# A two-layer attention and Mish-MLP block: norms handed out in eleven steps, heads inverted at other steps, two loads behind the attention

## The chip, the cores and the metric

The kernel runs on one core of a Trainium2 chip. The metric is the device time of one execution in microseconds (us), lower is better. A core has TensorE (PE, matmuls), VectorE (DVE), ScalarE (ACT), GpSimd (POOL) and SyncE (SP, which here only issues DMAs); each engine works through its own instructions in order, and they meet through semaphores.

## The reference

```python
def reference(A_x, A_wqkv, A_wo, B_x, B_w1, B_b1, B_w2):
    def _A_ref(x, wqkv, wo):
        ...
        scores = jnp.einsum("bhqd,bhkd->bhqk", q, k) * (Dh ** -0.5)
        p = _softmax(scores, axis=-1)
        o = jnp.einsum("bhqk,bhkd->bhqd", p, v)
        return (lambda x, *d: x.transpose(*d))(o, 0, 2, 1, 3).reshape(B, S, D) @ wo
    def _B_ref(x, w1, b1, w2):
        h = jnp.einsum("bsd,df->bsf", x, w1) + b1
        sp = jnp.log1p(jnp.exp(-jnp.abs(h))) + jnp.where(h > 0, h, jnp.zeros_like(h))  # stable softplus
        act = h * jnp.tanh(sp)
        return jnp.einsum("bsf,fd->bsd", act, w2)
    x = A_x
    x = x + _A_ref(_layernorm(x, axis=-1), A_wqkv, A_wo)
    x = x + _B_ref(_layernorm(x, axis=-1), B_w1, B_b1, B_w2)
    x = x + _A_ref(_layernorm(x, axis=-1), A_wqkv, A_wo)
    x = x + _B_ref(_layernorm(x, axis=-1), B_w1, B_b1, B_w2)
    return x
```

S = 2048 rows of D = 512, 32 heads of 16, F = 1792 hidden features, all float32. Both layers use the same weights.

## The kernel before, in words

**Tiles.** The 2048 rows are four tiles c = 0 to 3 of 512. Operands of the projections are split into a high and a low part in a reduced format (th and tl for a normed tile, oh and ol for an attention output, ah and al for an activation, two halves of every weight), and three matmuls replace one (`mm3`, L177). Weights are split once, in layer 0, kept in DRAM and loaded again as whole 1 MB tiles (`ready`, L159).

**The shared pool.** `b8` (L95) hands out tiles from one pool of 22 slots: q and k rows, the exponentials p, the heads' num and rec, oh and ol, weights, residuals x2 and normed tiles all take slots of it. A tile that takes a slot waits until the last reader of the tile before it is done, and a load that waits so holds the DMA queue that it stands in. Normalised rows on their way to DRAM and back share three buffers named raw.

**Order.** A scheduler places the instructions by a simulated time line. The kernel chains all matmuls of a stage in the order in which it writes them (`att.pe`) and pins others with `behind` (L118), which keeps pinned instructions of an engine in the program's order; an instruction that isn't pinned may be placed elsewhere.

**The stages of a layer.** Projections to q, k and v (`qkv`); attention over 8 groups of 4 heads and 4 query tiles; the output projection; the MLP. Attention is a loop of STEPS = 512 steps (`run`, L489): each works on 4 heads of 128 keys, in items P and S (scores of two heads or one, and their exponentials, L438 and L448), M (two matmuls for the running row maximum of a later step, and a VectorE reduce, L390) and v (p times v, L463). Maxima run 22 steps ahead, so they end 22 steps before the loop does. In the value projections before the loop a maximum is interleaved by `some_max`, at every third step. `hooks` is a table from step to functions that run behind that step's items; "STEPS-14" is the hook 14 steps before the end.

**The heads' way out** (`HeadsOut`, L630), for each row tile c: `load` brings the sums den and the outputs num back from DRAM (4 + 8 DMAs on SyncE), `invert` takes the reciprocal on VectorE (L647) and stores it through POOL's queue (4 DMAs, rscr, L649), `spread` loads it broadcast (8 DMAs on POOL's queue, rec, L655), `parts` multiplies (L659), casts on POOL (oh, L662) and subtracts (ol, L663), all 128x2048. For c = 0 to 2 these hang on hooks of the loop's last 42 steps. Tile 3 ends with the loop: its last output `ot` is stored by SyncE (L487) and loaded after the loop, inverted in the middle of projection 2, and `pieces` does its product and split in halves (L673, L674, L678) on the MLP's features 2 to 5.

**The output projection** (`wo_parts`, L681) has 16 steps of three matmuls a tile. Tiles 0 and 1 run whole, tile 2 for 10 steps (HEAD), with the first MLP norm (`norm_parts`, by PE transposes) drawn in between; the rest of tile 2 and all of tile 3 run inside the MLP. VectorE adds each half tile to the residual x2 (L701), which `load_res` has loaded.

**The MLP** (`mlp`, L705) goes over 4 tiles x 14 features: `hid` makes a hidden feature tile (12 matmuls) and a chain of ten ScalarE and VectorE operations over it, `outp` the output two features later (12 matmuls). Hooks here are keyed (c, f). The norm of the next row tile is made beside it by `norm_blocks` (L267), drawn by `spread` (L300) in six parts on six features in a row: statistics of all four subtiles; scaling, transposes and 4 DMAs of one half; the same of the other half; the load of the turned tile; two halves of the split (ScalarE L295, VectorE L296). In layer 0's last row tile three norms for the next layer's q and k are drawn as well, from features 1, 5 and 8.

Of the kernel before, what the change touches and what calls it, by code (L numbers as in the profile page):

```python
# [9 lines left out]
F32 = mybir.dt.float32  # L10
F32R = mybir.dt.float32r
BF16 = mybir.dt.bfloat16
AF = mybir.ActivationFunctionType
# [5 lines left out]
P = 128  # L19
# [31 lines left out]
MAX_M = (6, 3, 7)  # L51
T_BUFS = {"he": 1, "hr": 1}
NBLK = 22


def units(done):
# [12 lines left out]
def kernel(ctx: ExitStack, tc: tile.TileContext, x, wqkv, wo, w1, b1, w2, out):  # L69
# [48 lines left out]
    def behind(ins):  # L118
        return tc.keep_in_program_order(ins)
# [61 lines left out]
            pe(nc.tensor.matmul(acc, ah, bl, start=False, stop=False))  # L181
            pe(nc.tensor.matmul(acc, al, bh, start=False, stop=last and i == n - 1))  # L182

    def statistics(src, nm):
        st = tmp.tile([P, NCH, 6], F32, tag="st", name=f"st{nm}")
        mv = tmp.tile([P, NCH, 2], F32, tag="mv", name=f"mv{nm}")
        ve = tmp.tile([P, NCH], F32, tag="ve", name=f"ve{nm}")
        rs = tmp.tile([P, NCH], F32, tag="rs", name=f"rs{nm}")
        for t in range(NCH):
            behind(nc.vector.bn_stats(st[:, t], src[:, t]))  # L190
            behind(nc.vector.bn_aggr(mv[:, t], st[:, t]))
        nc.gpsimd.tensor_scalar(ve, mv[:, :, 1], EPS, None, op0=ALU.add)
        nc.gpsimd.tensor_tensor(rs, ve, mhalf, op=ALU.pow)
        return rs, mv

    def norm_parts(src, nm, got, key, tag, fine=False, pin=lambda ins: ins, pe=lambda ins: ins, halves=False):
        st = tmp.tile([P, NCH, 6], F32, tag="st", name=f"st{nm}")
        mv = tmp.tile([P, NCH, 2], F32, tag="mv", name=f"mv{nm}")
# [65 lines left out]
    def grouped(t):  # L264
        return t.rearrange("p (g j r) -> p g j r", j=2, r=TR)

    def norm_blocks(src, nm, got, key):  # L267
        rs, mv = statistics(src, nm)
        yield
        th = b8([P, KT, CW], F32R, f"th{nm}")  # L270
        tl = b8([P, KT, CW], F32R, f"tl{nm}")
        got[key] = (th, tl)
        raw = tl.bitcast(F32)
        turned = dram.tile([D, CW], F32, name=f"nt{nm}")
        for h in range(2):
            xn = tmp.tile([P, 2, D], F32, tag="raw", name=f"xn{nm}{h}", bufs=3)
            for j in range(2):
                t = h + 2 * j
                nc.vector.tensor_scalar(
                    xn[:, j], src[:, t], mv[:, t, 0:1], rs[:, t : t + 1], op0=ALU.subtract, op1=ALU.mult  # L280
                )
            y = tmp.tile([P, D // TR, 2, TR], F32, tag="raw", name=f"y{nm}{h}", bufs=3)
            for j in range(2):
                nc.vector.transpose(y[:, :, j], xn[:, j].rearrange("p (b r) -> p b r", r=TR))
            for a in range(P // TR):
                n0 = h * CW // 2 + a * 2 * TR
                nc.sync.dma_start(
                    turned[:, n0 : n0 + 2 * TR].rearrange("(b q) n -> q b n", q=TR),
                    y[ts(a, TR)].rearrange("q b j r -> q b (j r)"),
                )  # L290
            yield
        nc.sync.dma_start(raw, turned.rearrange("(k p) n -> p k n", p=P))
        yield
        for k in range(KT):
            nc.scalar.activation(th[:, k], raw[:, k], AF.Copy)  # L295
            nc.vector.tensor_tensor(tl[:, k], raw[:, k], th[:, k].bitcast(F32), op=ALU.subtract)  # L296
            if k % 2:
                yield

    def spread(hooks, c, f0, src, nm, got, key):  # L300
        parts = norm_blocks(src, nm, got, key)
        for i in range(6):
            hooks.setdefault((c, f0 + i), []).append(lambda: next(parts, None))

    class Attention:
        def __init__(self, l, scr):
# [231 lines left out]
    def qkv(l, att, wts, tt, order, within, due):  # L538
        scr = att.scr
        ahead = [0]  # L540

        def some_max():
            if ahead[0] < AHEAD + PRE:
                for n in range(2):
                    att.max_mm(ahead[0], n)
                ahead[0] += 1

        done = 0
        spare = []
        parts = iter(())  # L550
        for n, (m, c) in enumerate(order):
            for fn in within.get((n, 0), []):
                fn()
            w = wts[m // 2]
            if n % 2:
                if not spare:
                    two = b8([P, 2, 2, CW], F32R, f"pt{l}{m}{c}")
                    spare += [two[:, 0], two[:, 1]]
                pt = spare.pop(0)
            else:  # L560
                pt = tmp.tile([P, 2, CW], F32R, tag="raw", name=f"pt{l}{m}{c}", bufs=3)
            th, tl = tt[c]
            acc = pbank("s", f"qk{l}{c}{m}")
            if l == 0 and n < 2:
                for i, (part, t) in enumerate(((0, th), (0, tl), (1, th)) if n else ((0, th), (1, th), (0, tl))):
                    for k in range(KT):
                        start, stop = i == k == 0, i == 2 and k == KT - 1
                        att.pe(nc.tensor.matmul(acc, w[:, part, k, ts(m % 2, P)], t[:, k], start=start, stop=stop))
            for k in range(KT if l or n > 1 else 0):
                for fn in within.get((n, k), []) if k else []:  # L570
                    fn()
                mm3(
                    acc,
                    [(w[:, 0, k, ts(m % 2, P)], w[:, 1, k, ts(m % 2, P)], th[:, k], tl[:, k])],
                    first=k == 0,
                    last=k == KT - 1,
                    pe=att.pe,
                )
            split_psum(pt[:, 0], pt[:, 1], acc)
            nc.scalar.dma_start(  # L580
                scr[m][:, :, ts(c, CW)].bitcast(F32).rearrange("a p n -> p a n"), pt.bitcast(F32)
            )
            for fn in due.get((m, c), []):
                fn()
            for _ in range(2):
                next(parts, None)
            if m in (0, 4):
                done += 1
                if done == 2 * NCH:
                    parts = att.prep_qk(0)  # L590
                    for _ in range(2 * PREP):
                        next(parts)
            elif done == 2 * NCH and m in MAX_M:
                some_max()
        i = 0
        for c in range(NCH - 1):
            for _ in v_parts(l, c, wts, tt, att, False):
                i += 1
                if i % 3 == 2:
                    some_max()  # L600

    def v_parts(l, c, wts, tt, att, paired):
# [214 lines left out]
    for l in range(2):  # L817
# [24 lines left out]
        def load_res(c):  # L842
            x2 = b8([P, NCH, D], F32, f"x2{l}{c}")
            nc.sync.dma_start(x2, xsrc[ts(c, CW), :].rearrange("(t p) d -> p t d", p=P))
            x2s.append(x2)
# [9 lines left out]
        def at(s, fn):  # L855
            hooks.setdefault(s, []).append(fn)
# [6 lines left out]
                split_keep(hooks, 20 + 26 * i, key, *src)  # L863
        for i in range(2):
            at(STEPS - 9 + 2 * i, lambda i=i: wot.append(ready(f"wo{i}", l)))
            at(STEPS - 5 + 2 * i, lambda i=i: load_res(i))
        at(STEPS - 1, lambda: load_w1(0))
        outs = [HeadsOut(l, c, att.oscr) for c in range(NCH)]
        for c, (t0, t1, t2, t3) in enumerate(((-42, -21, -20, -14), (-26, -20, -19, -12), (-10, -6, -5, 0))):
            o = outs[c]  # L870
            at(STEPS + t0, o.load)
            at(STEPS + t1, o.invert)
            at(STEPS + t2, o.spread)
            at(STEPS + t3, lambda o=o: o.parts())
# [3 lines left out]

        att.run(hooks, v_parts(l, NCH - 1, wts, tt, att, True))
        outs[3].load()  # L880
        load_res(2)
        load_res(3)
        load_w1(1)
        load_w2(0)
        for _ in project(0):
            pass
        first = norm_parts(x2s[0], f"m{l}0", tts, 0, "s", pin=behind, pe=att.pe, halves=True)
        for i, _ in enumerate(project(1)):
            for n in range({0: 1, 8: 1, 11: 2, 14: 2}.get(i, 0)):
                next(first)  # L890
        last = project(2)
        for i in range(HEAD):
            next(last)
            for n in range({1: 2, 6: 1}.get(i, 0)):
                next(first)
            if i == 3:
                outs[3].invert()
                outs[3].spread()
        load_w1(2)
        load_w2(1)  # L900
        hooks = {}
# [16 lines left out]
            on(f1, lambda i=i: load_w1(i))  # L918
            on(f2, lambda i=i: load_w2(i - 1))
        on(9, lambda: load_w2(6))  # L920
        for c in range(NCH - 1):
            spread(hooks, c, 5 if c else 7, x2s[c + 1], f"m{l}{c + 1}", tts, c + 1)
        wts, tt = {}, {}
        if l == 0:
            end = NCH - 1
            for f, js in ((2, (0,)), (4, (2,)), (9, (1,)), (11, (3,)), (12, (4,)), (13, (5,))):
                hooks.setdefault((end, f), []).append(lambda js=js: load_qkv(1, wts, js, splits))
            for c in range(end):
                spread(hooks, end, (1, 5, 8)[c], x2s[c], f"q1{c}", tt, c)
        mlp(l, x2s, w1t, w2t, tts, xs if l == 0 else out, hooks, att.pe, last)  # L930
    close_banks()

# [27 lines left out]
```

## Time and profile before

| | us |
|---|---|
| median of 3 runs (lowest to highest) | 3543.35 (3543.12 to 3545.58) |
| the profiled execution | 3551.37 |
| its span in the profile | 3549.6 |

The profile is of one execution. Its times run from the span's start. A row of a group of instructions gives the line, the engine, the operation, what it writes and reads, the count, the busy time with the mean of one in ns, and the idle time of the engine just before them with what ended it. PE's ends are modelled, so overlapping matmuls show as 0.39 us each where one starts every 0.23 us. "Granted clock" is the share of TensorE's full clock.

| stage | layer 0, us from the start | layer 1 |
|---|---|---|
| q, k, v | 0 to 163 | 1790 to 1931 |
| attention | 163 to 1410 | 1931 to 3179 |
| output projections 0 to 2 | 1410 to 1444 | 3179 to 3211 |
| MLP | 1444 to 1790 | 3211 to 3545 |

### The profile page before, as it was taken

What the parts mean: (1) busy time and instruction counts of PE and PEld (TensorE: products, weight loads), DVE (VectorE), ACT (ScalarE), POOL (GpSimd) and SP (SyncE); (2) the same over time, 40 slices, a digit from 0 to 9 for tenths busy, and PEclk for the clock granted to TensorE, in tenths of its full rate; (3) what the DMA queues carried; (4) which work ended last, traced back from release to release, by engine and by line L of the source; (5) the groups of instructions that cost most, each with busy time, mean ns of one, the idle gap of its engine ahead of it and who ended that gap; (6) DMA issues with size and microseconds to landing.
All of it is one profiled execution on the core that took longest, in us unless ns stands there. A gap on an engine that the chain in (4) does not pass through costs nothing. (4 is left out here: it accounts for less than half of the span.)

```text
span 3549.6 us, 68828 instructions
## 1 busy us (share of the span) xinstructions
PE 3503.1 (99%) x28572; PEld 1932.6 (54%) x28572; DVE 3003.6 (85%) x3164; ACT 2578.2 (73%) x3515; POOL 242.9 (7%) x392
## 2 busy tenths in 40 slices
PE   9999999999999999899999999999999999999999
PEld 7644444444444444788776444444444444447887
DVE  6699999999999994577856999999999999945775
ACT  3288888888888887356522888888888888863665
POOL 3100001010000002100010000000000000020000
PEclk9999999999999999999999999999999999999999
DMA  7631322213132115621374211112111111165210
GB/s 247 228 92 47 83 52 69 56 55 71 44 80 50 41 21 119 193 72 47 107 236 153 48 34 43 38 29 44 32 35 37 43 35 29 21 136 180 80 36 24
DMA packets 182196, 273.97 MB, mean 77 GB/s; under 512 B 67508, under 2 KB 111476, under 8 KB 168060
## 3 DMA queue, kind: packets, MB, share of 16 engines
q1 hardware_dynamic: 154964, 192.91, 21.5%
q10 hardware_dynamic: 19176, 43.06, 3.5%
q0 software_dynamic: 7744, 33.60, 3.4%
q8 instruction: 224, 3.67, 0.5%
q14 instruction: 88, 0.72, 0.1%
HBM read 158.87 MB, written 109.58 MB: 76 GB/s over the span
## 5 line engine op out<-in xcount | busy, mean ns | idle before, releaser
L390 DVE TENSOR_REDUCE mxv<-pm 128x2 f32<-128x1024 f32 x2048 | 2383.3, 1219 | 144.6 <-PE pm L386 95.8
L438 ACT ACTIVATE p<-sp 128x1024 f32<-128x1024 f32 x1366 | 1395.7, 1022 | 18.4 <-DVE num L659 10.2
L463 PE MATMUL pv<-p,va 128*32 128x256 f32 (+2 forms) x16032 | 1169.6, 393 | 0.4 <-ACT ot L484 0.2
L386 PE MATMUL pm<-ks,qs 48*128 48x512 f32 x4096 | 1099.4, 447 | 1.6 <-DVE mxv L390 1.6
L448 ACT ACTIVATE p<-ss 128x512 f32<-128x512 f32 x1364 | 815.3, 598 | 344.7 <-PE ss L447 248.4
L437 PE MATMUL sp<-qs,ks 50*128 50x512 f32 x2732 | 741.5, 445 | 0.0
L386 PEld LDWEIGHTS pm<-ks,qs 48*128 48x128 f32 x4096 | 452.1, 184 | 351.3 <-issue 175.4
L463 PEld LDWEIGHTS pv<-p,va 128*32 128x32 f32 x16032 | 369.0, 109 | 502.9 <-issue 424.2
L447 PE MATMUL ss<-qs,ks 50*128 50x512 f32 x1364 | 613.1, 450 | 11.0 <-ACT p L448 11.0
L447 PEld LDWEIGHTS ss<-qs,ks 50*128 50x128 f32 x1364 | 252.5, 185 | 342.4 <-ACT p L448 235.0
L437 PEld LDWEIGHTS sp<-qs,ks 50*128 50x128 f32 x2732 | 270.4, 184 | 184.2 <-ACT p L438 110.2
L405 POOL CAST np<-nt 128x32 fp32r<-128x32 f32 x64 | 13.4, 210 | 2215.1 <-DVE nt L403 2215.1
L719 ACT ACTIVATE hb<-h,b1t 128x512 f32<-128x512 f32 x112 | 77.1, 689 | 94.3 <-PE h L182 91.7
L174 ACT ACTIVATE pt<-qk 128x512 fp32r<-128x512 f32 x64 | 38.3, 598 | 141.8 <-PE qk L182 101.5
L723 ACT ACTIVATE hr<-he 128x512 f32<-128x512 f32 x112 | 70.9, 633 | 89.6 <-DVE he L722 89.6
L726 DVE TENSOR_TENSOR hb<-hb,hr 128x512 f32<-128x512 f32 x112 | 77.2, 689 | 45.8 <-ACT hr L724 43.2
L729 ACT ACTIVATE ah<-hb 128x512 fp32r<-128x512 f32 x112 | 70.4, 629 | 57.5 <-DVE hb L726 44.3
L730 DVE TENSOR_TENSOR al<-hb,ah 128x512 fp32r<-128x512 f32 x112 | 77.2, 689 | 41.2 <-ACT ah L729 30.2
L720 DVE TENSOR_SCALAR he<-hb 128x512 f32<-128x512 f32 x112 | 47.6, 425 | 75.0 <-ACT hb L719 74.4
L722 DVE SCALAR_TENSOR_TENSOR he<-he 128x512 f32<-128x512 f32 x112 | 77.1, 688 | 21.0 <-ACT he L721 20.8
L175 DVE TENSOR_TENSOR pt<-qk,pt 128x512 fp32r<-128x512 f32 x64 | 43.9, 685 | 52.0 <-ACT pt L174 51.9
L721 ACT ACTIVATE he<-he 128x512 f32<-128x512 f32 x112 | 70.5, 629 | 22.7 <-DVE he L720 22.6
(237 smaller groups left out, 3090.8 us busy)
## 6 DMA issues: line engine op xcount, KB each, us to landing
scr<-pt ACTq DMA_DIRECT2D x64, 512.0 KB
qs<-scr SPq DMA_DIRECT2D x174, 128.0 KB
ks<-scr SPq DMA_DIRECT2D x174, 128.0 KB
vscr<-v SPq DMA_DIRECT2D x32, 512.0 KB
va<-vscr SPq DMA_DIRECT2D x64, 256.0 KB
oscr<-ot SPq DMA_DIRECT2D x64, 256.0 KB
ww<-sw POOLq DMA_DIRECT2D x14, 1024.0 KB, 4.6
num<-oscr SPq DMA_DIRECT2D x64, 128.0 KB
```

The costliest lines, as they stand in the source:

```text
L386: nc.tensor.matmul(pm[:, e], qs[u][rows, q0 : q0 + P], ks[u][rows, ts(n, 512)], start=True, stop=True)
L390: nc.vector.tensor_reduce(self.mxs[b][:, 2 * u : 2 * u + 2, qt, n], pm, axis=AX.X, op=ALU.max)
L437: self.pe(nc.tensor.matmul(sp[:, e], k, q, start=True, stop=True))
L438: nc.scalar.activation(self.pts[-1][:, 0:n], sp[:, 0:n], AF.Exp, scale=SCALE)
L447: self.pe(nc.tensor.matmul(sp, k, q, start=True, stop=True))
L448: nc.scalar.activation(self.pts[i // 3][:, 2], sp, AF.Exp, scale=SCALE)
L463: nc.tensor.matmul(self.accs[b][ts(h, VW), cols], self.va[b // NCH][:, kt, h, :], self.pts[j][:, e, cols], start=kt == 0 and q0 == 0, stop ...
L719: nc.scalar.activation(hb, acc, AF.Identity, bias=b1t[:, f : f + 1])
L722: nc.vector.scalar_tensor_tensor(e, e, 2.0, e, op0=ALU.add, op1=ALU.mult)
L723: nc.scalar.activation(r, e, AF.Ln, bias=1.0, scale=0.5)
L726: nc.vector.tensor_tensor(hb, hb, r, op=ALU.mult)
L730: nc.vector.tensor_tensor(low, full, high.bitcast(F32), op=ALU.subtract)
```

## The change

It has five parts. (1) `norm_blocks` becomes `norm_units`: the same operations, now all of VectorE's and ScalarE's pinned, in eleven units: four of statistics, four of scaling and transposing one subtile (the second and the fourth also issue 4 DMAs), the load, two halves of the split. Two tables say on which feature tile, counted 0 to 55 through the four row tiles, each unit runs. The slots for th and tl are taken at the load, no longer at the first scaling. (2) The hooks of load, invert, spread and parts of tiles 0 to 2 move; tile 3 is inverted and spread at step 6 of projection 1, no longer at step 3 of projection 2. (3) Of the loads, only residual 0 stays inside the loop; residual 1 and the first w1 tile go behind the loop and behind tile 3's load, and the order of the others changes. (4) The maxima in the value projections come one step later. (5) `statistics` goes into `norm_units`.

```diff
+M_NORMS = (
+    (3, 4, 5, 6, 6, 7, 8, 9, 10, 11, 11),
+    (14, 14, 15, 17, 18, 19, 20, 21, 22, 24, 25),
+    (31, 31, 32, 32, 32, 33, 34, 35, 36, 38, 39),
+)
+Q_NORMS = (
+    (22, 22, 23, 23, 26, 27, 28, 29, 43, 45, 48),
+    (36, 36, 37, 37, 40, 41, 42, 43, 50, 52, 53),
+    (46, 46, 47, 47, 48, 49, 50, 51, 53, 54, 55),
+)
...
-    def norm_blocks(src, nm, got, key):
-        rs, mv = statistics(src, nm)
-        yield
+    def norm_units(src, nm, got, key):
...
+        for t in range(NCH):
+            behind(nc.vector.bn_stats(st[:, t], src[:, t]))
+            behind(nc.vector.bn_aggr(mv[:, t], st[:, t]))
+            if t == NCH - 1:
+                nc.gpsimd.tensor_scalar(ve, mv[:, :, 1], EPS, None, op0=ALU.add)
+                nc.gpsimd.tensor_tensor(rs, ve, mhalf, op=ALU.pow)
+            yield
+        turned = dram.tile([D, CW], F32, name=f"nt{nm}")
+        for h in range(2):
+            xn = tmp.tile([P, 2, D], F32, tag="raw", name=f"xn{nm}{h}", bufs=3)
+            y = tmp.tile([P, D // TR, 2, TR], F32, tag="raw", name=f"y{nm}{h}", bufs=3)
+            for j in range(2):
+                t = h + 2 * j
+                behind(
+                    nc.vector.tensor_scalar(
+                        xn[:, j], src[:, t], mv[:, t, 0:1], rs[:, t : t + 1], op0=ALU.subtract, op1=ALU.mult
+                    )
+                )
+                behind(nc.vector.transpose(y[:, :, j], xn[:, j].rearrange("p (b r) -> p b r", r=TR)))
+                if j:
+                    for a in range(P // TR):
+                        n0 = h * CW // 2 + a * 2 * TR
+                        nc.sync.dma_start(
+                            turned[:, n0 : n0 + 2 * TR].rearrange("(b q) n -> q b n", q=TR),
+                            y[ts(a, TR)].rearrange("q b j r -> q b (j r)"),
+                        )
+                yield
         th = b8([P, KT, CW], F32R, f"th{nm}")
         tl = b8([P, KT, CW], F32R, f"tl{nm}")
...
         nc.sync.dma_start(raw, turned.rearrange("(k p) n -> p k n", p=P))
         yield
         for k in range(KT):
-            nc.scalar.activation(th[:, k], raw[:, k], AF.Copy)
-            nc.vector.tensor_tensor(tl[:, k], raw[:, k], th[:, k].bitcast(F32), op=ALU.subtract)
+            behind(nc.scalar.activation(th[:, k], raw[:, k], AF.Copy))
+            behind(nc.vector.tensor_tensor(tl[:, k], raw[:, k], th[:, k].bitcast(F32), op=ALU.subtract))
             if k % 2:
                 yield
 
-    def spread(hooks, c, f0, src, nm, got, key):
-        parts = norm_blocks(src, nm, got, key)
-        for i in range(6):
-            hooks.setdefault((c, f0 + i), []).append(lambda: next(parts, None))
+    def spread(hooks, when, src, nm, got, key):
+        parts = norm_units(src, nm, got, key)
+        for at in when:
+            hooks.setdefault(divmod(at, FT), []).append(lambda: next(parts))
...
-                if i % 3 == 2:
+                if i % 3 == 0:
                     some_max()
...
-            at(STEPS - 5 + 2 * i, lambda i=i: load_res(i))
-        at(STEPS - 1, lambda: load_w1(0))
+        at(STEPS - 4, lambda: load_res(0))
         outs = [HeadsOut(l, c, att.oscr) for c in range(NCH)]
-        for c, (t0, t1, t2, t3) in enumerate(((-42, -21, -20, -14), (-26, -20, -19, -12), (-10, -6, -5, 0))):
+        for c, (t0, t1, t2, t3) in enumerate(((-42, -38, -36, -21), (-26, -23, -22, -17), (-13, -9, -8, -1))):
...
         outs[3].load()
+        load_res(1)
+        load_w1(0)
         load_res(2)
+        load_w2(0)
+        load_w1(1)
         load_res(3)
-        load_w1(1)
-        load_w2(0)
...
             for n in range({0: 1, 8: 1, 11: 2, 14: 2}.get(i, 0)):
                 next(first)
+            if i == 6:
+                outs[3].invert()
+                outs[3].spread()
         last = project(2)
         for i in range(HEAD):
             next(last)
             for n in range({1: 2, 6: 1}.get(i, 0)):
                 next(first)
-            if i == 3:
-                outs[3].invert()
-                outs[3].spread()
...
-        for c in range(NCH - 1):
-            spread(hooks, c, 5 if c else 7, x2s[c + 1], f"m{l}{c + 1}", tts, c + 1)
+        for c, when in enumerate(M_NORMS):
+            spread(hooks, when, x2s[c + 1], f"m{l}{c + 1}", tts, c + 1)
...
-            for c in range(end):
-                spread(hooks, end, (1, 5, 8)[c], x2s[c], f"q1{c}", tt, c)
+            for c, when in enumerate(Q_NORMS):
+                spread(hooks, when, x2s[c], f"q1{c}", tt, c)
```

More of the change, by code (lines that the diff above doesn't have):

```diff
@@ L182, in mm3 @@
             pe(nc.tensor.matmul(acc, al, bh, start=False, stop=last and i == n - 1))
[L184 to L194, printed above, removed]
     def norm_parts(src, nm, got, key, tag, fine=False, pin=lambda ins: ins, pe=lambda ins: ins, halves=False):
@@ L265, in grouped @@
         return t.rearrange("p (g j r) -> p g j r", j=2, r=TR)
-    def norm_blocks(src, nm, got, key):
-        rs, mv = statistics(src, nm)
-        yield
+    def norm_units(src, nm, got, key):
+        st = tmp.tile([P, NCH, 6], F32, tag="st", name=f"st{nm}")
+        mv = tmp.tile([P, NCH, 2], F32, tag="mv", name=f"mv{nm}")
+        ve = tmp.tile([P, NCH], F32, tag="ve", name=f"ve{nm}")
+        rs = tmp.tile([P, NCH], F32, tag="rs", name=f"rs{nm}")
+        for t in range(NCH):
[25 more added lines that the diff above has]
+                yield
         th = b8([P, KT, CW], F32R, f"th{nm}")
@@ L273, in norm_blocks @@
         raw = tl.bitcast(F32)
[L274 to L291, printed above, removed]
         nc.sync.dma_start(raw, turned.rearrange("(k p) n -> p k n", p=P))
```

## The prediction

> **What bounds the kernel now.** I read the page's totals first, then the waits of TensorE, then busy time and granted clock stage by stage.
>
> ```profile
> span 3549.6 us, 68828 instructions
> ...
> PE 3503.1 (99%) x28572; PEld 1932.6 (54%) x28572; DVE 3003.6 (85%) x3164; ACT 2578.2 (73%) x3515; POOL 242.9 (7%) x392
> ...
> L390 DVE TENSOR_REDUCE mxv<-pm 128x2 f32<-128x1024 f32 x2048 | 2383.3, 1219 | 144.6 <-PE pm L386 95.8
> ```
>
> TensorE is busy for 3503.1 of 3549.6 us. No matmul is added or removed, so the change can only move the rest: time in which PE waits, and time in which it runs at a lower clock. The reduce row says who leads in the attention: VectorE waits for PE there (95.8 us over 2048 reduces).
>
> The waits of TensorE (total us, times, longest):
>
> ```profile
> PE mo L742 <- ACT ah L729: 13.0, 4, 4.6
> PE ss L447 <- ACT p L448: 11.0, 4, 5.5
> PE wo L182 <- DVE ol L678: 6.9, 2, 3.4
> PE wo L180 <- DVE x L701: 3.6, 2, 2.6
> PE pm L386 <- DVE mxv L390: 1.6, 2, 0.8
> ```
>
> Five causes hold 36.1 us. Where they lie (stretch, then PE, PEld, DVE, ACT, POOL busy, granted clock, DMA share, GB/s):
>
> ```profile
> 1386.80:1410.30 23.50, 17.97 (x179) 6.86 (x171) 5.45 (x3) 14.55 (x20) 7.97 (x13) 0.85 0.90 237
> 1410.30:1444.30 34.00, 31.38 (x147) 25.11 (x143) 18.61 (x24) 2.99 (x5) 5.27 (x7) 1.00 0.73 210
> 1444.30:1531.00 86.70, 78.36 (x329) 63.87 (x330) 50.73 (x84) 39.54 (x62) 5.37 (x10) 0.96 0.56 171
> 1636.00:1712.00 76.00, 76.00 (x337) 62.96 (x336) 55.41 (x97) 46.12 (x73) 2.03 (x2) 1.00 0.15 42
> 1712.00:1790.00 78.00, 72.05 (x304) 58.44 (x303) 62.33 (x117) 43.19 (x71) 5.83 (x6) 0.96 0.55 165
> 3153.00:3177.00 24.00, 19.21 (x158) 7.28 (x162) 5.45 (x3) 15.35 (x22) 7.97 (x13) 0.79 0.95 239
> 3211.40:3300.00 88.60, 81.31 (x333) 66.14 (x334) 51.62 (x86) 40.39 (x63) 5.38 (x10) 0.92 0.53 165
> ```
>
> The first three are layer 0's end of attention, projections and first MLP tile; then its third and fourth MLP tiles; then layer 1's end of attention and first MLP tile. An undisturbed MLP tile keeps PE busy for all its 76.00 us. The others lose idle time, and clock besides: seven stretches run at half clock, each begun by one of the long waits.
>
> ```profile
> 1392.70:1399.40 6.70, 5.07 (x30) 1.79 (x30) 3.16 (x2) 5.42 (x7) 3.02 (x4) 0.50 0.51 173
> ...
> 3256.40:3263.10 6.70, 5.62 (x13) 4.46 (x14) 2.32 (x3) 0.10 (x1) 0.00 (x0) 0.50 0.47 159
> sum 43.50, PE 38.72 PEld 23.90 DVE 24.55 ACT 24.34 POOL 5.44; mean PE 5.53 PEld 3.41 DVE 3.51 ACT 3.48 POOL 0.78
> ```
>
> In them PE works 38.72 us, of which half, 19.4 us, is lost. So about 36 + 19, some 55 us or 1.6%, is all that this change can win.
>
> **The change part by part.** First the heads of tiles 0 to 2, at the end of attention. VectorE in order of time, layer 0:
>
> ```profile
> 1358.24 1.77 DVE L647 RECIPROCAL den<-den 128x128 f32<-128x128 f32 x2
> 1373.68 2.29 DVE L659 TENSOR_TENSOR num<-num,rec 128x2048 f32<-128x2048 f32 x1 [13.68 <-DMA rscr<-den]
> 1381.91 2.29 DVE L663 TENSOR_TENSOR ol<-num,oh 128x2048 fp32r<-128x2048 f32 x1 [5.93 <-POOL oh L662]
> 1390.39 2.29 DVE L659 TENSOR_TENSOR num<-num,rec 128x2048 f32<-128x2048 f32 x1 [6.19 <-DMA num<-oscr]
> 1394.82 2.29 DVE L663 TENSOR_TENSOR ol<-num,oh 128x2048 fp32r<-128x2048 f32 x1 [2.14 <-POOL oh L662]
> 1397.03 0.95 DVE L647 RECIPROCAL den<-den 128x128 f32<-128x128 f32 x1
> 1416.11 2.29 DVE L659 TENSOR_TENSOR num<-num,rec 128x2048 f32<-128x2048 f32 x1 [18.13 <-PE wo L182]
> 1420.55 2.29 DVE L663 TENSOR_TENSOR ol<-num,oh 128x2048 fp32r<-128x2048 f32 x1 [2.14 <-POOL oh L662]
> ```
>
> ```profile
> 1392.77 1.02 ACT L438 ACTIVATE p<-sp 128x1024 f32<-128x1024 f32 x1 [5.57 <-DVE num L659]
> ```
>
> Here p is the exponential's tile, num the product and rec the spread reciprocal. Two reciprocals run back to back, and their chains (four rscr issues, a landing, eight rec issues, a landing, the product) go through POOL one after the other, so tile 1's product starts at 1390.39. An exponential needs a slot of the shared pool and gets it when that product ends, after 5.57 us; PE's longest "ss" wait is this one. With tile 0 inverted at STEPS-38, its 1 reciprocal, 12 POOL issues and later POOL cast are out of the way, and tile 1's chain runs alone. Tile 2's chain shows what it takes alone: 1397.03 to 1416.11, 19.1 us. From 1359.1 (second of the pair) tile 1's product would start at 1378.2 and end at 1380.5, while the exponential asks for the slot at 1392.77 - 5.57 = 1387.2: 6.7 us to spare. What goes is the idle time of the two stretches, 5.53 + 4.79, and half of the matmul time at half clock, 2.5 in layer 0 and, by 24.00 x 0.21, about 5.0 in layer 1: 17.9 us. Bounds 0 and 17.9; I take 16, near the top, as the margin exceeds the wait itself.
>
> Tile 2's reciprocal sits behind tile 1's product in VectorE's order. With that product 12.2 us sooner and the hook three steps sooner, I put it at 1385, its product at 1404 and ol (starting 4.44 later, by the last two rows) done by 1411. Attention would end at 1410.3 - 5.53 - 2.5 = 1402.3. Tile 2's load also moves three steps up, but reads what SyncE stores just ahead of it: nothing.
>
> The residual adds queue behind that ol, and PE waits for them, 3.6 us in both layers. In the projections 42 steps of three matmuls take 31.38 us, 0.75 each, so the second one wants its bank at 1402.3 + 12.0 = 1414.3; the add would end at 1412. Bounds 0 and 3.6; taken 3.
>
> Tile 0's reciprocal, 0.95 us, now lies among the reduces of the last block, where VectorE has 144.6 idle us in 2048 gaps. Bounds 0 and 0.95 a layer; taken 0.45, together 0.9 lost.
>
> Next tile 3's heads, and the loads. SyncE's queue in layer 0, and POOL and VectorE on what follows:
>
> ```profile
> 1418.43 0.34 SPq L164 DMA_DIRECT2D w10l<-ww  x1
> 1418.87 0.38 SPq L644 DMA_DIRECT2D num<-oscr  x1
> 1419.34 0.38 SPq L487 DMA_DIRECT2D oscr<-ot  x1
> ...
> 1426.38 1.94 SPq L641 DMA_DIRECT2D den<-oscr  x2
> ```
>
> ```profile
> 1441.09 2.08 POOL L649 DMA_DIRECT2D rscr<-den  x4 [11.32 <-DVE den L647]
> 1448.69 1.55 POOL L655 DMA_DIRECT2D rec<-rscr  x3 [5.52 <-DMA rscr<-den]
> ```
>
> ```profile
> 1470.97 1.23 DVE L673 TENSOR_TENSOR num<-num,rec 128x1024 f32<-128x1024 f32 x1 [7.89 <-DMA rec<-rscr]
> ```
>
> The first w1 load waits for tile 2's product (ends 1418.40), and behind it stands the store of the last attention output, 9 us after the loop's end at 1410.3. Moved behind tile 3's load, w1 and residual 1 hold nothing up: the store goes at about 1403, den 7 us later as now, at 1410. The reciprocal moves 13 steps up, to 1402.3 + 23 x 0.75 = 1419.5; its rscr issue at 1420.8. From rscr to product took 1441.09 to 1470.97, 29.9 us, which gives 1450.7. The product is wanted at 1470.97 - 7.89 = 1463.08, less the 8.0 and 2.6 gained, 1452.5. So the wait that starved PE twice (mo, then wo) is gone by only 1.8 us. At stake in the two first MLP tiles: idle 8.34 + 7.29, and of the 19.4 us of half clock what is left beside 2.5, 5.0 and 3.1 (78.00 x 0.04, fourth tile), 8.8: 24.4 us. Bounds 0 and 24.4; taken 17, because the margin is thin and the same weights still share the DMA engines.
>
> Residual 1 and w1 are now issued at about 1412 (0.4 us each of SyncE); the residual is first read half way through the second projection, 1402.3 + 24 x 0.75 = 1420.3. I cost them at nothing while that holds; the projections hide them.
>
> Then the norms. Their instructions stay the same in number; they are pinned and handed out one feature tile at a time. In layer 0's fourth tile three norms of the next layer meet: VectorE 62.33 busy us in 78, against 55.41 in 76, and
>
> ```profile
> 1765.81 0.63 ACT L295 ACTIVATE thq<-tlq 128x512 fp32r<-128x512 f32 x1 [4.38 <-DMA tlq<-ntq]
> ```
>
> ScalarE stands for 4.38 us before a split whose load has not landed. The change moves nearly all of two norms' statistics, scaling and transposes into the second and third tiles (the third's VectorE has 20 us free), and puts two feature tiles between load and split for tile 1. Idle 5.95 and clock 3.1 are at stake: bounds 0 and 9.0, taken 7.5. Pinning itself: a split that comes too early blocks ScalarE for later feature tiles. Bounds 0 and what the second rival says; taken 2 lost.
>
> Last, running maxima one step later in the value projections: the reduce before has one more step of three matmuls, some 0.75 us, to finish in, against two waits of 0.8. Bounds 0 and 1.6, taken 1.4.
>
> Sum: 16 + 3 - 0.9 + 17 + 7.5 - 2 + 1.4 = 42.0 us. The profiled execution took 3551.37 us with a span of 3549.6, the median of the runs shown is 3543.35; I take the saving off the median: **3501 us**.
>
> **The rivals.** *Tile 3's product stays late.* Loads that come sooner keep the engines full just then, and 1.8 us is nothing beside this spread:
>
> ```profile
> DMA to landing us min/median/max: 3.5/6.3/18.3
> ```
>
> The 17 stay lost: 25 us gained, 3518. For it the slowest rec landing, 18.3 us; against it the other landings' median, 6.3.
>
> The Trainium skill, page "DMA: Bandwidth & Descriptors", section "Queues, rings and completion order", says each DMA engine takes turns between the queues packet by packet, so POOL's megabyte would not wait behind SyncE's weights. At its 358 GB/s two megabytes take 5.9 us, an estimate from that page; by it this rival's chance would be 0.05 and the time still 3501. The 18.3 us here speak against so short a share.
>
> *Slower: pinned splits block.* One mechanism: a split whose load is late holds ScalarE, and every feature tile behind it. The 4.38 us wait is followed by the stage's longest idle time, at most 5.95, and its half clock, 3.1; I price it at 6.5, some 70% of both. Nine norms pay it if loads land after the splits' places: 58.5 lost, 42 + 2 gained, 3558. It turns the sign from the seventh norm on. For it: half of tile 1's split in the MLP comes a feature tile sooner. Against it: all other splits keep their distance from the load or get a feature tile more.
>
> *The wait moves.* Residual 1 lands after 1420.3; the add, the first norm's scaling and PE's transposes stand behind it. Eight us late with half clock behind it is 12 a layer: 3501 + 24 = 3525. For it: at the attention end's 237 GB/s a megabyte takes 4.4 us, and it is second after tile 3's own, 1421 from 1412.
>
> *The slot is another's.* The exponential may get a slot with a later release; then the 16 stay lost: 3517. Against it: the exponential's row names that product, and it starts 0.1 us after its end.
>
> **How the numbers follow.** Forecast 0.50, with its own range 3490 to 3508 (all 55 gained, and the taken sum less 7); product late 0.18; wait moves 0.13; other slot 0.11; slower 0.08. The range reaches from 3489 to 3527 to take in the three middle cases and leaves out the slower one and pairs of them. A difference under 0.2%, 7 us, can't be told from none: pairs of the middle cases come there, 0.06; so faster 0.86, slower 0.08.
>
> **What would show it.** Right: no "ss" wait on p near either layer's attention end, tile 1's product near 1378; the store of the last output issued within 2 us of the loop's end; product L673 starting without a DMA wait; clock 1.00 in the stretches above; the fourth MLP tile without idle PE. Wrong: L673 still waiting on rec; transposes L257 waiting behind residual 1; "mo" waits beside a pinned split in MLP tiles that had none.

## The result, and the profile after

| | before | after |
|---|---|---|
| median of 6 runs each, taken together (lowest to highest), us | 3544.47 (3540.85 to 3548.10) | 3527.52 (3526.25 to 3534.03) |
| the profiled execution, us | 3551.37 | 3526.25 |
| its span, us | 3549.6 | 3524.4 |

The ratio is 0.9955, with a 95% interval from 0.9943 to 0.9968: faster by 17 us, where 42 were forecast. The 3527.52 us lie just above the range's 3527, and the forecast of 3501 is 26 us off.

From here on the line numbers are those of the changed kernel: the lines of before named here stand 10 further down. TensorE's work and its waits (total us, times, longest) in the profile after; "pv" is p times v, "ss" the scores of one head, "mo" the MLP's output, "wo" the output projection and "pm" the running maxima:

```profile
span 3524.4 us, 68795 instructions
...
PE 3492.5 (99%) x28572; PEld 1925.5 (55%) x28572; DVE 3003.6 (85%) x3164; ACT 2575.0 (73%) x3515; POOL 239.2 (7%) x392
```

```profile
PE pv L473 <- ACT p L448: 10.2, 2, 5.7
PE wo L192 <- DVE ol L688: 8.1, 2, 4.0
PE ss L457 <- ACT p L458: 1.7, 3, 0.8
```

Of the five waits of before, those of "mo" for ah and of "wo" for the residual sums are gone, and that of "pm" for the maxima is down from 1.6 us to 0.4. The wait of "ss" for an exponential is mostly gone by name only: "pv" now waits for one, for 10.2 us, and "ss" still for 1.7, where it was 11.0. "wo" for ol is larger than before. Stage by stage (stretch, then PE, PEld, DVE, ACT, POOL busy, granted clock, DMA share, GB/s; the same five parts of layer 0 as before, then the half-clock stretches):

```profile
1386.10:1409.40 23.30, 18.76 (x186) 7.39 (x182) 4.59 (x2) 15.20 (x21) 5.96 (x9) 0.89 0.59 178
1409.40:1440.90 31.50, 31.50 (x143) 25.80 (x143) 13.89 (x22) 2.99 (x5) 7.88 (x14) 0.97 0.95 314
1440.90:1527.60 86.70, 82.38 (x355) 67.38 (x354) 53.90 (x89) 42.42 (x66) 1.28 (x2) 0.98 0.48 146
1622.90:1698.90 76.00, 75.81 (x335) 62.48 (x334) 60.29 (x110) 45.68 (x74) 3.08 (x4) 1.00 0.25 70
1699.60:1777.60 78.00, 77.82 (x344) 64.09 (x343) 60.02 (x106) 46.22 (x77) 2.23 (x4) 1.00 0.49 159
```

```profile
1404.30:1411.10 6.80, 5.21 (x22) 2.56 (x23) 2.72 (x2) 3.03 (x4) 1.89 (x1) 0.50 0.02 6
...
3233.80:3237.20 3.40, 3.40 (x10) 2.63 (x9) 2.37 (x6) 0.00 (x0) 0.23 (x1) 0.51 0.81 270
sum 20.50, PE 15.56 PEld 9.00 DVE 11.44 ACT 5.68 POOL 5.30; mean PE 3.89 PEld 2.25 DVE 2.86 ACT 1.42 POOL 1.33
```

The fourth MLP tile went from 72.05 busy us in 78 to 77.82, and the first from 78.36 of 86.70 to 82.38. The attention's end is as it was: 18.76 busy of 23.30, against 17.97 of 23.50. What the two long waits left cost, in both layers together, is 10.2 + 8.1 us of waiting and half of the 15.56 at half clock, some 26 us. That this is also the distance to the forecast is in part chance, as the part on the prediction shows. They are these, the exponential of the last pair but one in each layer and the projection of tile 3 (here in layer 0):

```profile
1404.81 1.02 ACT L448 ACTIVATE p<-sp 128x1024 f32<-128x1024 f32 x1 [5.94 <-DVE num L669]
...
3157.57 1.02 ACT L448 ACTIVATE p<-sp 128x1024 f32<-128x1024 f32 x1 [7.08 <-DVE num L669]
```

```profile
1481.52 0.50 PE L192 MATMUL wo<-wo1l,ol 128*128 128x512 f32 x1 [4.04 <-DVE ol L688]
```

And VectorE and POOL on the way to the first:

```profile
1373.57 2.29 DVE L669 TENSOR_TENSOR num<-num,rec 128x2048 f32<-128x2048 f32 x1 [2.05 <-DMA rec<-rscr]
1378.00 2.29 DVE L673 TENSOR_TENSOR ol<-num,oh 128x2048 fp32r<-128x2048 f32 x1 [2.13 <-POOL oh L672]
1380.21 0.94 DVE L657 RECIPROCAL den<-den 128x128 f32<-128x128 f32 x1
1402.43 2.29 DVE L669 TENSOR_TENSOR num<-num,rec 128x2048 f32<-128x2048 f32 x1 [21.28 <-DMA rec<-rscr]
```

```profile
1381.45 1.99 POOL L659 DMA_DIRECT2D rscr<-den  x4 [3.48 <-DVE den L657]
1391.96 4.06 POOL L665 DMA_DIRECT2D rec<-rscr  x8 [8.52 <-ACT p L458]
```

Tile 1's product starts at 1373.57, sooner even than the 1378.2 forecast, and no exponential waits for it any more. But the last pair but one is now given the slot (called buffer here) of tile 2's spread reciprocals, free when tile 2's product ends: 1402.43 + 2.29 = 1404.72. The exponential starts 0.1 us later. The prediction had that product at 1404, and did not ask whose buffer it frees.

### The profile page after: what moved, and what is told of

Its sections match the earlier page's. It is cut to its first block, busy times and chain, and to the rows that moved or that the text cites. A ratio compares the mean times of both kernels' runs of the same rounds, so it can differ in the third digit from the quotient of the medians.

```text
span 3524.4 us, 68795 instructions
## 1 busy us (share of the span) xinstructions
PE 3492.5 (99%) x28572; PEld 1925.5 (55%) x28572; DVE 3003.6 (85%) x3164; ACT 2575.0 (73%) x3515; POOL 239.2 (7%) x392
## 3 DMA queue, kind: packets, MB, share of 16 engines
q1 hardware_dynamic: 154964, 192.91, 21.5%
## 5 line engine op out<-in xcount | busy, mean ns | idle before, releaser
L473 PE MATMUL pv<-p,va 128*32 128x256 f32 (+2 forms) x16032 | 1169.9, 393 | 11.6 <-ACT p L448 10.2
L734 ACT ACTIVATE hr<-hr,lnhalf 128x512 f32<-128x512 f32 x112 | 81.1, 724 | 3.5
```

Source lines behind the costliest of these rows:

```text
L473: nc.tensor.matmul(self.accs[b][ts(h, VW), cols], self.va[b // NCH][:, kt, h, :], self.pts[j][:, e, cols], start=kt == 0 and q0 == 0, stop ...
L734: nc.scalar.activation(r, r, AF.Exp, bias=lnhalf, scale=-1.0)
```

## The experiments

Each is an edit of the changed kernel; us are medians (lowest to highest, number of runs). "Ratio" is to the kernel before, with its 95% interval; the kernel before, timed beside them, had medians of 3544.62 to 3547.37. The changed kernel itself, run again beside two of them:

> The changed kernel itself, beside the others of this call: 3526 to 3530, so that differences of 2 us between calls are not read as effects.

3528.56 (3526.78 to 3532.46, 5), ratio 0.9951 [0.9938, 0.9964].

**Another buffer for the last exponentials.**

```diff
-        for c, (t0, t1, t2, t3) in enumerate(((-42, -38, -36, -21), (-26, -23, -22, -17), (-13, -9, -8, -1))):
+        for c, (t0, t1, t2, t3) in enumerate(((-42, -38, -36, -21), (-26, -23, -22, -17), (-13, -9, -5, -1))):
```

> The changed kernel with one number different: tile 2's reciprocals are spread behind step STEPS-5 instead of STEPS-8. The order of instructions on every engine is the same; only the buffer that the spread reciprocals lie in differs, so the second-to-last pair's exponential no longer has to wait for tile 2's product. Slot theory: in the profile of the changed kernel that exponential started 0.1 us after tile 2's product (1402.43 to 1404.72) and PE stood for 4.54 us at 1405.89 and 5.69 us at 3158.65, with 6.8 us of half clock around each. Both stalls go; per layer 4.5 to 5.7 us of standing and about 3 us of lost clock, 14 to 17 us in all, of which some returns as a later wait: 3512 to 3520 us beside a median of 3527 for the changed kernel, and the idle time of the pair's exponential (L448) before a DVE product is under 1 us. Rival, the chain is late whichever buffer it is in: PE stops a few us later for tile 2's product or for the residual sums, and the time stays within 3 us of 3527.

3512.81 (3510.59 to 3529.00, 6), ratio 0.9914 [0.9900, 0.9929]. Layer 0, VectorE and then the attention's end (columns as above):

```profile
1402.92 2.29 DVE L669 TENSOR_TENSOR num<-num,rec 128x2048 f32<-128x2048 f32 x1 [22.04 <-PE pv L473]
```

```profile
1386.10:1402.50 16.40, 16.40 (x182) 6.49 (x180) 0.00 (x0) 14.85 (x21) 4.06 (x8) 1.00 0.90 254
```

Tile 2's product comes no sooner (1402.92 against 1402.43), but the loop does not wait for it: PE is busy for all 16.40 us, at full clock. So the chain was not too late for its use, only for a buffer that it did not need to share. The prediction's 16 us lay here; the edit wins 14.7.

**The order of tile 3's pieces.**

```diff
-        for f in range(2, 6):
+        for f in range(1, 5):
             on(f, lambda: next(pieces))
```

> The changed kernel with the four pieces of tile 3's product taken behind features 1 to 4 instead of 2 to 5. Order theory: the wait of tile 3's projection for ol (4.04 us in each layer, with 3.4 us of half clock behind it, at 1481.5 and 3233.5) comes from where the last piece stands in VectorE's order (it ran at 1480.24, PE asked at 1477.5), not from data; a feature is about 5.5 us, so the piece is then some 2.7 us ahead of the demand and the wait goes: 3 to 6 us per layer, 3515 to 3521 us. Rival, the data is late: the first product at feature 1 waits for the spread reciprocals (landed at 1439 in the changed kernel) or for VectorE, which pushes the hidden features behind it, and the same 4 us come back as waits of mo for ah: 3524 to 3530.

3516.30 (3515.22 to 3518.43, 5), ratio 0.9918 [0.9906, 0.9930]. The last piece ran at 1480.24 in the changed kernel, when PE stood; here:

```profile
1456.28 1.23 DVE L683 TENSOR_TENSOR num<-num,rec 128x1024 f32<-128x1024 f32 x1 [3.47 <-issue]
...
1476.64 1.22 DVE L688 TENSOR_TENSOR ol<-num,oh 128x1024 fp32r<-128x1024 f32 x1
```

In the kernel with the edit no wait for DMA stands before the first piece, and the waits of "wo" for ol are gone in both layers. The data was there: the wait was one of order.

**Both.**

> Both edits together. If the two stalls are separate, the gains add: 3500 to 3512 us. If one is only the other seen later (tile 3's product is late because the attention ended late), the sum is no better than the better of the two.

3500.34 (3499.88 to 3501.26, 4), ratio 0.9873 [0.9859, 0.9888]. The gains add (14.7 + 11.2 = 25.9 expected from 3527.5, 27.2 found). TensorE's longest waits, and the clock:

```profile
PE warm L815 <- DVE warm L810: 1.4, 1, 1.4
PE ss L457 <- ACT p L458: 1.2, 2, 0.6
PE mo L752 <- ACT ah L739: 0.9, 2, 0.6
```

```profile
core 0: 3498.4 us, clock 1.000
```

This version is faster than the kernel before and the changed one.

**One part undone at a time.** The loads first (residuals 0 and 1 at STEPS-5 and STEPS-3, w1 at STEPS-1):

```diff
-        at(STEPS - 4, lambda: load_res(0))
+            at(STEPS - 5 + 2 * i, lambda i=i: load_res(i))
+        at(STEPS - 1, lambda: load_w1(0))
...
-        load_res(1)
-        load_w1(0)
         load_res(2)
-        load_w2(0)
-        load_w1(1)
         load_res(3)
+        load_w1(1)
+        load_w2(0)
```

> The changed kernel with the loads where they were: the residuals of tiles 0 and 1 at STEPS-5 and STEPS-3, w1's first pair at STEPS-1, the others behind the loop in the old order. Theory: the loads' place decides when the last output's store and tile 3's chain start (store 1419.3 before, 1410.2 after), and whether the first sums wait for residual 1. Back come the residual waits (3 us) and most of the 17 us of tile 3's late product, about 9 us a layer of which 3 or 4 are covered by the earlier reciprocal; the exponential that waits for tile 2's product is one pair earlier, so that stall grows by 1 to 2 us a layer: 3540 to 3550 us. Rival: what cured tile 3's lateness is the earlier reciprocal (in the middle of tile 1's projection); then the loads are worth only the 3 us of the residual sums: 3527 to 3533.

3542.66 (3539.14 to 3545.56, 11), ratio 0.9993 [0.9984, 1.0001]: as much as theory said, for another reason. ScalarE, layers 0 and 1:

```profile
1410.89 1.02 ACT L448 ACTIVATE p<-sp 128x1024 f32<-128x1024 f32 x1 [12.49 <-DVE num L669]
```

```profile
3171.05 1.03 ACT L448 ACTIVATE p<-sp 128x1024 f32<-128x1024 f32 x1 [14.15 <-DVE num L669]
```

The wait at the attention's end doubles, by far more than the 1 to 2 us expected; neither the residual waits nor the late product of tile 3 come back. Tile 2's product is what comes later, in layer 0 with these rows (VectorE, then the eight loads of rec, issued from 1392.85 on):

```profile
1408.51 2.29 DVE L669 TENSOR_TENSOR num<-num,rec 128x2048 f32<-128x2048 f32 x1 [26.39 <-DMA x<-in_A_x_dram]
```

```profile
DMA to landing us min/median/max: 6.5/9.1/11.9
```

In the changed kernel these eight loads took 6.2/6.5/6.9 us. The loads that the edit puts back into the loop are issued just ahead of them, between 1387 and 1398, and VectorE's row names one of them. That they share the DMA engines with rec fits; no run takes it apart further.

Then tile 3's reciprocal (back to step 3 of tile 2's projection), and the norms (old blocks for all tiles, at their old features):

```diff
-            if i == 6:
-                outs[3].invert()
-                outs[3].spread()
...
+            if i == 3:
+                outs[3].invert()
+                outs[3].spread()
```

> The changed kernel with tile 3's reciprocal and its spread back in tile 2's projection, all else kept. In the changed kernel the reciprocal ran at 1425.85 and the first piece of tile 3's product at 1460.01 without a wait for DMA. Theory: the reciprocal's place alone cured that wait. It then runs near 1438, the chain of 30 us behind it ends near 1468, 8 us after the demand: mo waits for ah 4 us in each layer, with half clock behind it, 8 to 14 us in all: 3535 to 3541. Rival: the earlier store of the last attention output (1410.16 instead of 1419.34) cured it, or shares the cure: under 5 us, 3527 to 3532.

3527.45 (3525.29 to 3530.88, 5), ratio 0.9947 [0.9934, 0.9959]: no difference, the rival's case. The reciprocal ran at 1436.05; the first piece, on VectorE:

```profile
1461.13 1.23 DVE L683 TENSOR_TENSOR num<-num,rec 128x1024 f32<-128x1024 f32 x1 [1.83 <-DMA rec<-rscr]
```

VectorE waits 1.83 us for the spread reciprocals, PE not at all.

> The changed kernel with the old norms in the MLP phase (statistics at once, blocks of six, next(parts, None) at features 5 or 7 on, and 1, 5, 8 of the last tile) and everything else of the change kept. Theory: the new norms are worth what the fourth MLP tile of layer 0 lost (85.98 us before, 75.79 after) less what the pinned small steps cost in the second and third (75.68 and 76.16 before, 77.46 and 76.64 after): the fourth tile goes back to 84 to 86 us, the second to 75.7; 6 to 9 us slower than the changed kernel, 3533 to 3537 us. Rival: the fourth tile lost its time to the lateness that it inherited from earlier in the layer, and the norms are worth 0 to 3 us: 3527 to 3530.

3533.94 (3532.21 to 3535.28, 5), ratio 0.9963 [0.9951, 0.9976]: 6.4 us, the theory's case. PE waits again in the fourth MLP tile of layer 0 and after it, at the three places of before (1.25, 1.14 and 3.56 us there) and once behind the tile:

```profile
1738.57 2.11 PE L752 MATMUL mo<-w23l,ah 128*128 128x512 f32 x8 [1.08 <-ACT ah L739]
1741.82 1.20 PE L752 MATMUL mo<-w23l,al 128*128 128x512 f32 x4 [1.14 <-DVE al L740]
1760.16 1.20 PE L752 MATMUL mo<-w25l,al 128*128 128x512 f32 x4 [1.73 <-DVE al L740]
1787.76 0.50 PE L190 MATMUL qk<-thq,qkv0l 128*128 128x512 f32 x1 [1.91 <-DVE pt L185]
```

Together they are 5.86 us, near the 5.95 us idle of before; the granted clock there was 1.00, so the half clock of before did not come back, and the longest wait is shorter than its 3.56.

The maxima (`i % 3 == 2`), and the heads' times:

> The changed kernel with the maxima beside the values at every third step from the third on (i % 3 == 2), as before. Theory: the two waits of pm for mxv (0.79 us each) return, 1.6 us slower: 3528.5 to 3530. Rival: both attention loops of the changed kernel are 0.7 and 1.4 us longer than before from their first score to the last maximum, and the maxima's place is the cause: 0 to 2 us faster than the changed kernel, 3525 to 3528.

3529.91 (3528.28 to 3532.30, 5), ratio 0.9953 [0.9939, 0.9966]. Both waits of 0.79 us were back, but 1.4 to 2.4 us above the two medians of the changed kernel, with overlapping runs, don't settle a size.

```diff
-        for c, (t0, t1, t2, t3) in enumerate(((-42, -38, -36, -21), (-26, -23, -22, -17), (-13, -9, -8, -1))):
+        for c, (t0, t1, t2, t3) in enumerate(((-42, -21, -20, -14), (-26, -20, -19, -12), (-10, -6, -5, 0))):
```

> The changed kernel with the old times of the heads' output in the attention (tiles 0 to 2 loaded, inverted, spread and multiplied at the old steps), the new order of loads kept. No exponential then gets the buffer of tile 2's reciprocals; one gets that of tile 1's, as before. Theory: the sooner heads moved the stall from tile 1's product (5.53 and 4.62 us) to tile 2's (4.54 and 5.69 us) and won nothing there; what they give is that tile 2's product is not behind the first residual sums. So the old stall of about 5 us a layer returns in place of the new one: 3524 to 3532. Rival: the sooner heads are what the changed kernel's gain rests on; without them tile 2's product comes after the projection's start and the sums wait: 3532 to 3545.

3535.67 (3526.86 to 3536.13, 5), ratio 0.9963 [0.9951, 0.9976]: the rival's range, though the theory's wait is there (5.79 us of ScalarE, behind tile 1's product). On top of it the sums come late behind tile 2's product, PE waits 1.65 us for one in layer 1, and its transposes wait 1.02 and 1.78 us behind them. One of the five runs took 3526.86, in the theory's range.

**Several parts undone.** Tile 3's product had stayed in time in all of these, so they were undone together:

> Loads and tile 3's reciprocal both as before, the rest of the change kept. Each alone left no wait of mo for ah. Theory: the two are two cures of one wait, either is enough, so with both undone the first MLP tile loses it again (110.8 and 111.8 us before, 104.4 and 104.6 with the loads alone back): 6 to 9 us in each layer on top of the loads' 3542.7, 3551 to 3560. Rival: something else in the change cures it (the sooner product of tile 2, which clears VectorE for the sums): within 4 us of 3542.7.

3542.59 (3541.13 to 3544.97, 11), ratio 0.9991 [0.9982, 1.0000], the rival's case: not these two.

> Loads and the heads' times as before; tile 3's earlier reciprocal, the norms and the maxima of the change kept. Theory on the attention's end: the sooner heads and the moved loads cancel each other there. With both back the long wait is 4.6 to 5.5 us again, as before, and not the 12 to 14 us of the loads alone back. The residual sums wait again (3.6 us), and tile 3's chain starts late, because the first w1 load stands ahead of the last output's store until tile 2's product: the wait of mo for ah is back, shortened by the earlier reciprocal to 0 to 4 us a layer. 3532 to 3542. Rival: no cancelling, the loads alone make the wait: 12 us or more stay, 3545 to 3552.

3531.16 (3526.54 to 3538.83, 6), ratio 0.9964 [0.9952, 0.9976]. The time lies just under the theory's 3532 to 3542, PE waits 2.3 us for one residual sum, and the "mo" wait stays away. But the long waits are near before's, and not 12 to 14 us, which is the theory on the attention's end. ScalarE, layers 0 and 1:

```profile
1391.44 1.02 ACT L448 ACTIVATE p<-sp 128x1024 f32<-128x1024 f32 x1 [4.85 <-DVE num L669]
```

```profile
3144.61 1.02 ACT L448 ACTIVATE p<-sp 128x1024 f32<-128x1024 f32 x1 [6.26 <-DVE num L669]
```

The wait is for tile 1's product again. Tile 2's rec, with the old hooks, is issued from 1404.34 on, well behind these loads, and lands in 4.3/5.5/6.1 us.

> Loads, heads' times and tile 3's reciprocal as before: the kernel before with the new norms and maxima alone. Theory: all three parts have to be back for tile 3's product to be late again, because each of them alone puts that chain ahead of its demand; first MLP tiles of 110 to 112 us, mo waits for ah 3.5 us or more in both layers, and the time is that of the kernel before less the norms (6.4) and the maxima (1.6): 3535 to 3540. Rival: the new norms of the MLP tiles cured it themselves: the first MLP tiles stay at 104.5, 3522 to 3530.

3539.73 (3534.73 to 3544.69, 11), ratio 0.9982 [0.9973, 0.9990], the theory's case. Only here does "mo" wait again for longer than 1.1 us; PE's waits, the first piece, and the landings of rec ahead of it:

```profile
PE mo L752 <- ACT ah L739: 6.5, 2, 3.8
```

```profile
1469.62 1.22 DVE L683 TENSOR_TENSOR num<-num,rec 128x1024 f32<-128x1024 f32 x1 [7.11 <-DMA w23l<-ww]
```

```profile
DMA to landing us min/median/max: 6.5/12.6/17.5
```

VectorE's row names the load of a weight, which the product doesn't read; the last of rec's eight loads was issued at 1451.70 and took the 17.5 us.

Last, in the kernel with both edits, the old norms for MLP tiles 1 to 3:

> The kernel with both edits (slot_and_pieces, 3500.3) and with the old norms for MLP tiles 1 to 3; the norms of the next layer in the last MLP tile stay in the new eleven steps. Theory: the pinned small steps cost 1.8 and 0.5 us in layer 0's second and third MLP tiles and 0.24 in layer 1's second, and win nothing for these tiles: 3497.3 to 3499. Rival: the old blocks hold VectorE long enough beside tile 3's pieces to bring a wait back in the first MLP tile: 3501 to 3506.

3499.25 (3497.86 to 3500.01, 4), ratio 0.9867 [0.9853, 0.9881]. About 1 us with runs that touch: these tiles' norms win nothing by the small steps, and lose hardly anything.

## Why the prediction was wrong, point by point

**The step that failed** is "Bounds 0 and 17.9; I take 16, near the top, as the margin exceeds the wait itself". It measured the margin to tile 1's product alone. That product is in time, as said, and the rival "The slot is another's" took place all the same, with its 16 us: the exponentials go round one pool of 22 buffers, and the same edit that moved tile 1's product moved tile 2's load and spread three steps up, so that the last pair but one meets tile 2's buffer. The rival had 0.11 because one row of before named one product. A list of every tile that shares the pool, with the time at which each gives its buffer back, was called for.

**Heads and loads cancel there.** The sooner heads with the old loads gave 12.49 and 14.15 us; the old heads with the old loads 4.85 and 6.26; both new 5.94 and 7.08 (ScalarE's idle time). Undone alone, the two cost 8 and 15 us; together only 3.6 (3531.16 against 3527.52, with runs that overlap). In part the loads' move is a repair of what the sooner heads did: they bring tile 2's rec to where the old loads are issued. The prediction added the two as if they were separate.

**Tile 3's late product, 17 of 24.4 taken.** Two waits were put together as one cause. That of "mo" for ah went in both layers, and the first MLP tiles won about 12 us: idle time from 15.6 to 8.7 (4.32 above; 4.33 in layer 1, 82.77 busy of 87.10), lost clock from 8.8 to about 3.3 (82 x 0.02, twice). It has more margin than the 1.8 us worked out: the chain is in time with the old reciprocal, with the old loads, with both, or with the old heads; of the sets tried, only with all three back is it late (the heads with the reciprocal were not tried without the loads). So no single edit is its cause, and experiments that undo one part each could not show one. With the early reciprocal rec's slowest load still took 17.4 us, but the loads start 14 us sooner than before (1434.76 against 1448.69) and land in time. With the late one, in layer 0, it took 12.4 us (reciprocal back) and 7.1 (loads too) where the wait was cured, and where not 17.5 (three parts back) and 18.3 (before); the first issue to the first piece took 16.3 and 14.7 us against 21.5 and 22.3. That the neighbouring weight loads are issued sooner, by rec's time, in the cured cases fits, but was not tried alone, so this cause stays open. That of "wo" for ol stayed, and with its half clock was worth 11.2 us: an order of pieces that this change doesn't touch. The rival of a late product did not happen, though its slow landing, 18.3 us before, did.

**The base.** The terms were read from an execution 8 us above the median and taken off the median. The profiled pair differs by 25.1 us, the medians by 17.0. Of the 26 us of error 8 are this step, an estimate, as no trace shows which waits a median run had shorter. Some 13 are the attention's end, where the long waits stayed (10.3 us before, 10.2 after) and only 3 us of half clock went, in layer 1. Some 5 are tile 3's. The other terms about cancel.

**What held.** The norms: 7.5 taken, 6.4 found. The residual sums: 3 taken, and no wait of "wo" for them after. The store of the last output went 0.6 us behind its tile (1409.54, 1410.16), with w1's load behind it at 1416.79. Residual 1 came in time. No pinned split blocked an MLP tile, so the slower case and its sign fell; the 2 us for pinning were about 1 or less. The maxima's two waits of 0.8 went.

**Luck.** The forecast's 3501 is near the time of the kernel with the two waits taken away, 3500.34, by chance: between the two profiled spans that kernel won 51.2 us (3549.6 to 3498.4), 9 more than the 42 forecast, and the 8 us of the base hide them.

## What to carry to other kernels

Where a pool of buffers is shared, moving a tile's allocation moves the waits of everything that comes round behind it: list who gets each buffer after the edit, and when it is given back, before a stall is called gone. Here one spread three steps later, with the same order of instructions on every engine, was worth 15 us. A saving read from one execution is taken off that execution's own time, and two waits that follow each other are two terms until each has its own cause.

## What the runs showed of the hardware

The runs lie closest where no long wait is left. The kernel with both edits has a granted clock of 1.000, and its four runs lie within 1.4 us (2.2 with the old norms); those of the other kernels lie 3 to 18 us apart. The spread does not go by the size of the waits, though: with loads and reciprocal back, where PE waits 27.9 us for exponentials, it is 3.8 us. It is 18 with the later spread, where one run took 3529.00 at a clock of 0.993 and the others had 0.998 or 0.999. The half clock comes in pieces of about 3.4 us or a multiple: 6.8, 3.4, 6.9 and 3.4 us in the profile after. The Trainium skill, page "TensorE: Matmul & The Clock Gate", section "Part 1: The HAM clock gate", has the clock either half or full, set by an activity window of about 3.4 us, and half after a window of idling; these lengths agree. A piece came without any wait of that length too, in layer 1 of the kernel with the later spread, where PE's waits in the 10 us ahead and the piece itself were 0.43, 0.68 and 0.34 us:

```profile
3119.74:3126.57 6.83, 6.49 (x46) 2.24 (x43) 3.17 (x3) 5.41 (x7) 3.12 (x4) 0.50 0.59 101
```

That piece cost 3.2 us (half of 6.49). What began it is open: in the changed kernel, at the same place of the loop, PE waited 0.28, 0.68 and 0.83 us, and the clock stayed at 1.00:

```profile
3117.57:3134.40 16.83, 15.05 (x154) 5.66 (x158) 7.74 (x4) 14.95 (x22) 6.28 (x8) 1.00 0.62 100
```

So a stretch can lose clock without a long wait, and the sum of its short ones does not say whether it will.
